# One in-order load queue for activations and weights, weight casts on GpSimd, transposes issued from ScalarE, in a retention plus MLP kernel on one core

## The chip, the cores and the metric

The kernel runs on one core of a Trainium2 chip. The metric is device time in microseconds (us), the median of several executions. Engine names in the profile: PE is TensorE's matmul row, PEld its weight loads, DVE is VectorE, ACT is ScalarE, POOL is GpSimd, SP is SyncE. A name with q (SPq, ACTq) is that engine's instruction queue where it issues DMAs. "L83" is a line of the kernel's file.

## The reference

```python
scores = q @ k.T / sqrt(64)                      # batch 8, heads 8, sequence 576, head_dim 64
ret    = scores * Dmat                           # Dmat[i,j] = gamma_h ** (i-j) for i >= j, else 0
x      = (ret @ v) -> (4608 tokens, 512)
h      = x @ w_in                                # 512 x 2048
g      = h * tanh(softplus(h))                   # "mish"
out    = g @ w_out                               # 2048 x 512, float32
```

Inputs and output are float32. The kernel computes in bf16 with float32 accumulation.

## The kernel before

The 4608 tokens are cut into 36 chunks of 128; four chunks (0 to 3, 4 to 7, ...) make a tile of 512 tokens, nine tiles in all. A chunk goes through four steps: P (GpSimd casts k and scales v, VectorE scales q), T (q and k are transposed), S (score matmuls, mask on VectorE, state matmul) and O (output matmuls, copy into the tile's `xT`). A tile then goes through `g1`, the first MLP layer (16 blocks f of 4 matmuls and one activation on ScalarE), and `g2`, the second layer (16 groups of 4 matmuls, an output copy and a store per chunk). In the main loop, tile t's `g1`, tile t-1's `g2` and the attention of tile t+1 are interleaved.

```python
io  = tile_pool("io",  bufs=8)    # raw q, k, v: 8 chunks deep
tok = tile_pool("tok", bufs=3)    # cast q, k, v of a chunk
op  = tile_pool("op",  bufs=3)    # "res": output copies on their way to HBM
PF = 7
for n in range(PF): load(n)       # each load: 3 DMAs of 256 KB on SyncE's queue
# ... constants ...
def load_w_in(i):                 # float32 -> bf16 in the DMA, on GpSimd's queue
    nc.gpsimd.dma_start(out=w_in_t[:, :, ts(i, 512)], in_=w_in_r[:, :, ts(i, 512)])
# ...
def step_t(n):
    # ...
    if n < NCH:                   # chunks 0 to 3: 8 PE transposes into PSUM, copied by ScalarE
        tp = ps_o.tile([P, 2 * NP, P], BF16, name="ops")
        for i in range(2 * NP):
            nc.tensor.transpose(tp[:, i, :], flat[:, ts(i, P)], ident)
        nc.scalar.copy(qk.rearrange("p i n t -> p (i n) t"), tp)
    else:                         # all others: a DMA transpose, on SyncE's queue
        nc.sync.dma_start_transpose(out=qk.rearrange("p i n t -> p (i n) t"), in_=flat)
# ...
        if step == "P":
            prep(n); step_t(n)
            if n + PF < n_chunks: load(n + PF)
# ...
for i in range(4): load_w_in(i)
for n in range(NCH):
    att(n, "P"); att(n, "S"); att(n, "O")
for i in range(4): load_w_out(i)
att(NCH, "P")
for t in range(nT + 1):
    # per i of 16: P of chunk n+1 and S of chunk n (i%4 == 0), O of n (i%4 == 2), g1(t, i), g2(t-1, i)
```

## Time and profile before

| | before |
|---|---|
| time | 364.15 us median (363.94 to 366.07, 4 runs) |
| span of the profiled run | 362.2 us |
| PE busy | 303.6 us (84%) |
| first MLP matmul | 67.53 us |
| tile 1 begins in the main loop | 88.0 us |

The busy row of PE over the span in 40 equal slices of about 9 us (a digit is tenths), with the TensorE clock that was granted and the mean share of the DMA engines:

```profile
PE   1134200699999999999999999999999999999994
...
PEclk9999999999999999999999999999999999999998
DMA  8999999999866977677777786677322222110022
```

The stretch before the first MLP matmul (7 slices and a bit) is nearly empty on PE while the DMA engines are full. After it PE is busy all the time. The wait that ends this stretch, by the timeline (start us, duration us, engine, line, operation; in brackets the idle time of the engine before it and what ended it):

```profile
62.05 2.21 SPq L166 DMA_TRANSPOSE qkT<-qks  x1
...
66.59 0.61 PE L176 MATMUL sc<-qkT 64*128 64x128 bf16 x8 [27.70 <-DMA qkT<-qks]
...
67.53 1.06 PE L228 MATMUL hp<-xT,w_in_t 128*128 128x512 bf16 x2
```

PE idled 27.7 us before the scores of chunk 4, for chunk 4's DMA transpose (L166). That was issued at 62.05, though its input had been ready since 40.2 (VectorE's scaling of chunk 4's q, from 39.53; GpSimd's cast of its k was done at 33.6): on SyncE's queue it stood behind the loads of chunks up to 10.

In the groups view (busy us and mean ns of one, then the idle time before the group and what ended most of it):

```profile
L228 PE MATMUL hp<-xT,w_in_t 128*128 128x512 bf16 x576 | 148.2, 382 | 0.0
L238 PE MATMUL ops<-w_out_t,gT 128*128 128x512 bf16 x576 | 145.2, 379 | 0.0
...
L176 PE MATMUL sc<-qkT 64*128 64x128 bf16 x288 | 15.4, 231 | 32.5 <-DMA qkT<-qks 28.1
```

The two MLP layers are 1152 matmuls whose starts are 0.216 us apart in a full loop: 249 us that no reordering takes away. What can shrink is the stretch before 67.5.

### The profile page before, as it was taken

The numbers are of one execution on the slowest core, as the hardware profiler recorded it, in microseconds if no ns is written. First come the engines' busy times: TensorE is split into PE (matmuls) and PEld (weight loads), VectorE is DVE, ScalarE is ACT, GpSimd is POOL, SyncE is SP. The second block draws the span as 40 slices with busy tenths as digits, with TensorE's granted clock in tenths as the row PEclk, the third lists the DMA queues.
The fourth block names the chain that finished last, engine by engine and source line by source line (L and its number), as shares of the span: only waits on it lengthen the run. The fifth ranks groups of instructions, "written<-read, shape, count | busy, mean of one in ns | idle before, by whom it ended". The sixth has DMA issues, their size and how long they took to land.

```text
span 362.2 us, 5007 instructions
## 1 busy us (share of the span) xinstructions
PE 303.6 (84%) x2016; PEld 146.7 (40%) x2016; DVE 135.6 (37%) x188; ACT 93.0 (26%) x152; POOL 77.0 (21%) x92
## 2 busy tenths in 40 slices
PE   1134200699999999999999999999999999999994
PEld 1123100354444444444444444444444444444442
DVE  2324400376444444554444444445444444300121
ACT  2012100144322323232322323223322323233300
POOL 7037020133223222222222222222222200000000
PEclk9999999999999999999999999999999999999998
DMA  8999999999866977677777786677322222110022
GB/s 153 196 219 208 194 211 211 222 186 218 162 158 140 200 164 153 147 146 176 171 157 169 169 172 150 147 152 172 80 65 58 61 58 60 29 59 29 29 89 58
DMA packets 155800, 50.67 MB, mean 140 GB/s; under 512 B 147073, under 2 KB 151169, under 8 KB 155777
## 3 DMA queue, kind: packets, MB, share of 16 engines
q1 hardware_dynamic: 151552, 46.15, 61.3%
q0 software_dynamic: 4224, 4.19, 6.9%
q8 instruction: 16, 0.26, 0.3%
q14 instruction: 8, 0.06, 0.1%
HBM read 36.70 MB, written 9.44 MB: 127 GB/s over the span
## 4 chain that ended last, share of the span: by engine, by line
PE 78%; SPq 16%; DMA 3%; issue 1%; DVE 1%; DVEq 0%
PE ops L238 34%; PE hp L228 34%; SPq L83 15%; PE ot L209 3%; PE sc L176 3%; DMA qkT<-qks 3%; PE st L190 3%; PE ot L204 1%; SPq L87 1%; DVE qks L152 0%; DVE res L242 0%; SPq L166 0%; DVEq L152 0%; DVE xT L217 0%
## 5 line engine op out<-in xcount | busy, mean ns | idle before, releaser
L228 PE MATMUL hp<-xT,w_in_t 128*128 128x512 bf16 x576 | 148.2, 382 | 0.0
L238 PE MATMUL ops<-w_out_t,gT 128*128 128x512 bf16 x576 | 145.2, 379 | 0.0
L230 ACT ACTIVATE gT<-hp 128x512 bf16<-128x512 f32 x144 | 86.0, 597 | 220.1 <-PE hp L228 220.1
L238 PEld LDWEIGHTS <-gT 128*128 128x128 bf16 x576 | 56.4, 98 | 68.0
L228 PEld LDWEIGHTS <-w_in_t 128*128 128x128 bf16 x576 | 52.6, 98 | 57.2 <-issue 1.7
L242 DVE COPY res<-ops 128x512 f32<-128x512 f32 x36 | 24.9, 692 | 116.0 <-PE ops L238 110.3
L180 DVE TENSOR_TENSOR sm<-sc,mask 128x1024 bf16<-128x1024 f32 x36 | 43.9, 1220 | 47.8 <-PE sc L176 47.8
L153 POOL TENSOR_TENSOR vs<-vraw,gv 128x512 bf16<-128x512 f32 x36 | 38.0, 1056 | 97.8 <-PE ot L209 74.2
L151 POOL CAST qks<-kraw 128x512 bf16<-128x512 f32 x36 | 31.2, 866 | 113.6 <-PE st L190 76.5
L217 DVE CAST xT<-ot 128x512 bf16<-128x512 f32 x36 | 24.9, 692 | 53.2 <-PE ot L209 52.7
L176 PE MATMUL sc<-qkT 64*128 64x128 bf16 x288 | 15.4, 231 | 32.5 <-DMA qkT<-qks 28.1
L152 DVE TENSOR_TENSOR qks<-qraw,gq 128x512 bf16<-128x512 f32 x36 | 26.5, 737 | 3.5 <-DMA qraw<-in_q_dram 3.5
L176 PEld LDWEIGHTS <-qkT 64*128 64x128 bf16 x288 | 8.7, 99 | 47.0 <-DMA qkT<-qks 28.8
L213 DVE TENSOR_TENSOR ssb<-st,diag 128x512 bf16<-128x512 f32 x32 | 21.8, 682 | 0.0
L163 PE MATMUL ops<-ident,qks 128*128 128x128 bf16 x32 | 4.5, 309 | 19.6 <-DVE qks L152 12.4
L209 PE MATMUL ot<-sm,vs 128*64 128x128 bf16 x288 | 15.8, 234 | 1.9 <-DVE sm L180 1.9
L190 PE MATMUL st<-vs,qks 128*128 128x128 bf16 x128 | 13.8, 235 | 0.0
L209 PEld LDWEIGHTS <-vs 128*64 128x64 bf16 x288 | 10.2, 114 | 7.8 <-issue 5.5
L204 PEld LDWEIGHTS <-ssb 128*128 128x128 bf16 x128 | 9.3, 103 | 5.9
L204 PE MATMUL ot<-qkT,ssb 128*128 128x128 bf16 (+1 forms) x128 | 11.6, 221 | 0.0
L164 ACT COPY qkT<-ops 128x1024 bf16<-128x1024 bf16 x4 | 4.0, 1012 | 29.3 <-PE ops L163 29.3
L163 PEld LDWEIGHTS <-qks 128*128 128x128 bf16 x32 | 2.9, 135 | 20.9 <-DVE qks L152 13.1
(24 smaller groups left out, 20.7 us busy)
## 6 DMA issues: line engine op xcount, KB each, us to landing
qraw<-in_q_dram SPq DMA_DIRECT2D x32, 256.0 KB, 3.9
kraw<-in_k_dram SPq DMA_DIRECT2D x32, 256.0 KB, 4.4
vraw<-in_v_dram SPq DMA_DIRECT2D x32, 256.0 KB, 4.7
out_dram<-res SPq DMA_DIRECT2D x32, 256.0 KB, 2.1
w_in_t<-in_moe_w_in_dram POOLq DMA_DIRECT2D x4, 512.0 KB, 11.8
w_out_t<-in_moe_w_out_dram POOLq DMA_DIRECT2D x4, 512.0 KB, 11.6
qraw<-in_q_dram SPq DMA_DIRECT2D x8, 128.0 KB, 3.4
kraw<-in_k_dram SPq DMA_DIRECT2D x8, 128.0 KB, 3.4
```

Of the source, the lines that this page charges most:

```text
L83: nc.sync.dma_start(out=t, in_=src[b, :, ds(P * c, P), :].rearrange("h p d -> p h d"))
L151: nc.gpsimd.tensor_copy(qks[:, 1], kr)
L152: nc.vector.tensor_tensor(qks[:, 0], qr, gq[:, c, :].unsqueeze(2).to_broadcast([P, H, D]), op=OP.mult)
L153: nc.gpsimd.tensor_tensor(vs, vr, gv[:, c, :].unsqueeze(2).to_broadcast([P, H, D]), op=OP.mult)
L176: nc.tensor.matmul(sc[:, e, p, :], lhsT=qk[r, 1, p, :], rhs=qk[r, 0, p, :], start=True, stop=True)
L180: nc.vector.tensor_tensor(sm.rearrange("p e n i -> p (e n) i"), sc.rearrange("p e n i -> p (e n) i"), m.unsqueeze(1).to_broadcast([P, 2 * ...
L209: nc.tensor.matmul(ot[ds(64 * e, 64), p, :], lhsT=vs[:, 2 * p + e, :], rhs=sm[:, e, p, :], start=(first and p == 0), stop=True, skip_group ...
L217: nc.vector.tensor_copy(xts[t][:, :, ts(s, P)], ot)
L228: nc.tensor.matmul(hp, lhsT=w_in_t[:, c, ts(f, P)], rhs=xts[t][:, c, :], start=(c == 0), stop=(c == KC - 1))
L230: nc.scalar.activation(gts[t][:, f, :], hp, AX.Mish)
L238: nc.tensor.matmul(ops, lhsT=gts[t][:, f, ts(s, P)], rhs=w_out_t[:, f, :], start=(f == 0), stop=(f == nF - 1))
L242: nc.vector.tensor_copy(ot, ops)
```

## The change

Intent: fill the first 67 us. All loads go out in order on one queue, first chunks 0 to 3, then `w_in` in eight pieces of 512 KB, then chunks and `w_out` pieces mixed; the pieces stay float32 and GpSimd casts them. Tile 0 consumes the weights as they come, also in its second layer: four accumulators (two PSUM buffers of `ops` and two of `hp`) take one `w_out` row block after another, while the attention of tile 1 runs. DMA transposes move to ScalarE's queue so as not to stand behind loads. The diff is shortened; `...` marks what is left out or abridged.

```diff
+    stage = ctx.enter_context(tc.tile_pool(name="stage", bufs=STG))      # STG = 4
+    def load_w(nm, i):                 # one 512 KB piece, float32, SyncE's queue
+        t = stage.tile([P, 1024], F32, name="wst")
+        ... nc.sync.dma_start(out=t..., in_=w_in_r[:, :, ts(i, 256)]  or  w_out_r[:, ts(i, 2), :])
+    def cast_w(nm, i):
+        ... nc.gpsimd.tensor_copy(w_in_t[:, :, ts(i, 256)]  or  w_out_t[:, ts(i, 2), :], ...)
-    for n in range(PF):
+    for n in range(NCH):
         load(n)
+    for i in range(STG):
+        load_w("in", i)
...
-            nc.sync.dma_start_transpose(out=qk.rearrange("p i n t -> p (i n) t"), in_=flat)
+            nc.scalar.dma_start_transpose(out=qk.rearrange("p i n t -> p (i n) t"), in_=flat)
...
         if step == "P":
             prep(n)
+            if n >= 2 * NCH - 1 and n + PF < n_chunks:
+                load(n + PF)           # P of chunks 7 and 8 loads chunks 14 and 15
...
+    for i in range(8):
+        cast_w("in", i)
+        if i + STG < 8: load_w("in", i + STG)
+        g1(0, 2 * i); g1(0, 2 * i + 1)
+    load(4); att(4, "P"); att(4, "T")
+    for i in range(STG):
+        load_w("out", i)
+        if i % 2: load(4 + (i + 1) // 2)
+    def more(j, n):
+        cast_w("out", j)
+        if j + STG < 8: load_w("out", j + STG)
+        if j == 1: load(7)
+        elif j == 3:
+            for m in range(2 * NCH, 2 * NCH + 4): load(m)
+        elif j in (4, 6): load(2 * NCH + 2 + j // 2)
+    for f in range(nF):                # second layer of tile 0, with attention of tile 1
+        ... w == 0: more, S(n)   w == 1: P(n+1)   w == 2: more, O(n)   w == 3: T(n+1)
+        for s in range(NCH):
+            nc.tensor.matmul(accs[s], lhsT=gts[0][:, f, ts(s, P)], rhs=w_out_t[:, f, :], ...)
+    for s in (2, 3, 0, 1):             # four output copies and stores of tile 0
+        store(0, s, accs[s], nc.vector.tensor_copy if s % 2 else nc.scalar.copy)
+    for t in range(1, nT + 1):         # the main loop, from tile 1; T(n+1) at i%4 == 1; g2 from t = 2
```

More of the change, by code (lines that the diff above doesn't have):

```diff
@@ L64 @@
     op = ctx.enter_context(tc.tile_pool(name="op", bufs=3))
+    STG = 4
+    stage = ctx.enter_context(tc.tile_pool(name="stage", bufs=STG))
     PS = bass.MemoryType.PSUM
@@ L91, in load @@
         raw[n] = tiles
+    w_in_t = wpool.tile([P, KC, d_ff], BF16)
+    w_out_t = wpool.tile([P, nF, d_model], BF16)
+    w_in_r = moe_w_in.rearrange("(c p) f -> p c f", p=P)
+    w_out_r = moe_w_out.rearrange("(f p) d -> p f d", p=P)
+    staged = {}
+    def load_w(nm, i):
+        t = stage.tile([P, 1024], F32, name="wst")
+        if nm == "in":
+            nc.sync.dma_start(out=t.rearrange("p (c f) -> p c f", c=KC), in_=w_in_r[:, :, ts(i, 256)])
+        else:
+            nc.sync.dma_start(out=t.rearrange("p (f d) -> p f d", f=2), in_=w_out_r[:, ts(i, 2), :])
+        staged[nm, i] = t
+    def cast_w(nm, i):
+        t = staged.pop((nm, i))
+        if nm == "in":
+            nc.gpsimd.tensor_copy(w_in_t[:, :, ts(i, 256)], t.rearrange("p (c f) -> p c f", c=KC))
+        else:
+            nc.gpsimd.tensor_copy(w_out_t[:, ts(i, 2), :], t.rearrange("p (f d) -> p f d", f=2))
     PF = 7
-    for n in range(PF):
+    for n in range(NCH):
         load(n)
+    for i in range(STG):
+        load_w("in", i)
     ident = consts.tile([P, P], BF16)
@@ L126 @@
     nc.vector.memset(diag[64:P, 64:P], 1.0)
-    w_in_t = wpool.tile([P, KC, d_ff], BF16)
-    w_out_t = wpool.tile([P, nF, d_model], BF16)
-    w_in_r = moe_w_in.rearrange("(c p) f -> p c f", p=P)
-    w_out_r = moe_w_out.rearrange("(f p) d -> p f d", p=P)
-    def load_w_in(i):
-        nc.gpsimd.dma_start(out=w_in_t[:, :, ts(i, 512)], in_=w_in_r[:, :, ts(i, 512)])
-    def load_w_out(i):
-        nc.gpsimd.dma_start(out=w_out_t[:, ts(i, 4), :], in_=w_out_r[:, ts(i, 4), :])
     st_ps = {}
@@ L240, in g2, with store @@
         if part == 3:
-            ot = op.tile([P, d_model], F32, name="res")
-            nc.vector.tensor_copy(ot, ops)
-            b, c = chunks[NCH * t + s]
-            if c < 4:
-                nc.sync.dma_start(out=out[ds(b * S + P * c, P), :], in_=ot)
-            else:
-                for e in range(2):
-                    nc.sync.dma_start(out=out[ds((b + e) * S + 512, 64), :], in_=ot[ds(64 * e, 64), :])
+            store(t, s, ops, nc.vector.tensor_copy)
+    def store(t, s, ops, copy):
+        ot = op.tile([P, d_model], F32, name="res")
+        copy(ot, ops)
+        b, c = chunks[NCH * t + s]
+        if c < 4:
+            nc.sync.dma_start(out=out[ds(b * S + P * c, P), :], in_=ot)
+        else:
+            for e in range(2):
+                nc.sync.dma_start(out=out[ds((b + e) * S + 512, 64), :], in_=ot[ds(64 * e, 64), :])
     n_chunks = len(chunks)
@@ L257, in att @@
             prep(n)
+            if n >= 2 * NCH - 1 and n + PF < n_chunks:
+                load(n + PF)
+        elif step == "T":
             step_t(n)
-            if n + PF < n_chunks:
-                load(n + PF)
         elif step == "S":
@@ L264, in att @@
             step_o(n)
-    for i in range(4):
-        load_w_in(i)
     for n in range(NCH):
-        att(n, "P")
-        att(n, "S")
-        att(n, "O")
-    for i in range(4):
-        load_w_out(i)
-    att(NCH, "P")
-    for t in range(nT + 1):
+        for step in "PTSO":
+            att(n, step)
+    for i in range(8):
+        cast_w("in", i)
+        if i + STG < 8:
+            load_w("in", i + STG)
+        g1(0, 2 * i)
+        g1(0, 2 * i + 1)
+    load(4)
+    att(4, "P")
+    att(4, "T")
+    for i in range(STG):
+        load_w("out", i)
+        if i % 2:
+            load(4 + (i + 1) // 2)
+    accs = [ps_o.tile([P, d_model], F32, name="ops") for _ in range(2)]
+    accs += [ps_h.tile([P, NCH * P], F32, name="hp") for _ in range(2)]
+    def more(j, n):
+        cast_w("out", j)
+        if j + STG < 8:
+            load_w("out", j + STG)
+        if j == 1:
+            load(7)
+        elif j == 3:
+            for m in range(2 * NCH, 2 * NCH + 4):
+                load(m)
+        elif j in (4, 6):
+            load(2 * NCH + 2 + j // 2)
+    for f in range(nF):
+        n, w = NCH + f // 4, f % 4
+        if w == 0:
+            more(f // 2, n)
+            att(n, "S")
+        elif w == 1:
+            att(n + 1, "P")
+        elif w == 2:
+            more(f // 2, n)
+            att(n, "O")
+        else:
+            att(n + 1, "T")
+        for s in range(NCH):
+            nc.tensor.matmul(accs[s], lhsT=gts[0][:, f, ts(s, P)], rhs=w_out_t[:, f, :],
+                             start=(f == 0), stop=(f == nF - 1))
+    for s in (2, 3, 0, 1):
+        store(0, s, accs[s], nc.vector.tensor_copy if s % 2 else nc.scalar.copy)
+    for t in range(1, nT + 1):
         for i in range(nF):
@@ L282 @@
                     att(n, "S")
+                elif w == 1:
+                    att(n + 1, "T")
                 elif w == 2:
@@ L285 @@
                 g1(t, i)
-            if t > 0:
+            if t > 1:
                 g2(t - 1, i)
```

## The prediction

> **What bounds it now.** Two phases. The 40-slice view shows PE at 9 tenths from about 68 us on, and nearly nothing before. By the timeline tile 0's first MLP matmul starts at 67.5 us and the second tile's interleaved loop at 88.8; from there PE is 100% busy (stage table: 50.00 of 50.00 us in 200:250), a tile with attention takes about 32.3 us, the matmul chain ends near 357.7, the last store 4.5 us later.
>
> The first 67 us are mostly waiting. Weight loads on the GpSimd queue compete with chunk 1, whose attention starts at 14.7, chunk 0's at 4.2. Attention of four chunks ends at 39.6 (6.1 us each once data is there, a serial chain). Then PE idles 27.7 us, put down in the groups view to "DMA qkT<-qks": the transpose of chunk 4 sits on SyncE's queue behind loads of later chunks and issues at 62.05, landing at 66.5. A 786 KB chunk then takes about 3.5 us (213 GB/s).
>
> **What the change does.** Bytes read stay the same. Weights come as 512 KB fp32 pieces, cast by GpSimd (the 512-element k cast takes 0.61 us alone, 1.01 beside VectorE; estimate for 1024 elements 1.2 to 1.9 us, 16 casts). Transposes no longer queue behind loads, but hold ScalarE 1.24 us each (its SyncE duration; up to 2.7 loaded), in order with the activations.
>
> My timeline, an estimate from these durations:
> - Chunks 0 to 3 land by about 16.5 us, attention ends near 30 (the 6.1 us chain limits, not loading).
> - w_in pieces[...] are cast by about 33, hardly limiting: the first layer of tile 0 runs 30 to 46 (16 x 0.865, plus about 2 cold).
> - Chunk 4's transpose stands behind the last activation on ScalarE: issued near 47, landed near 50.5: PE idles 4 us and restarts cold. The Trainium skill ("TensorE: Matmul & The Clock Gate", Part 1) says the clock halves after about 3.4 us idle; this trace agrees: six matmuls took 2.75 us at 67.5, later 0.216 each.
> - Second layer of tile 0 with attention of tile 1: 4.8 us of PE work per chunk, but the next transpose waits for q-scale after the mask (2.5 us) and lands 3.2 to 5 us later, so 6 to 6.5 us per chunk. It ends near 76. w_out's last cast is near 66: weights limit less than this chain.
> - Tile 1's first layer alone: 4.8 us of work, 6 with the transpose on ScalarE: until about 101.
> - Then six full tiles (194), 27.7, 13.9 and the 4.5 tail: 240.
>
> Sum 341 us of span; time exceeds span by 1.7, but my stalls are rounded up: 341.5. So about 27.7 us of MLP second-layer and overlapped attention work moves into time that was idle, and some 5 to 8 us are given back as transpose latency. The steady loop should be unchanged: its transpose has 8 us per chunk.
>
> **Predicted: 341.5 us, 80% range 333 to 350. Faster by over 2%: 0.95; within 2%: 0.04; slower: 0.01.**
>
> **Signs.** Right: first MLP matmul near 30 us; idle before score matmuls released by the qkT transpose of some 4 us once and 1 to 2 us per chunk until about 100; span after that equal to before; few waits of PE on w_in or w_out casts. Wrong: accumulating matmuls waiting on GpSimd casts (weights limit), or the interleaved loop over 8.1 us per chunk (ScalarE held up).
>
> **What would break it.** Transposes landing in 6 us or more beside a full load queue (350); weight pieces slower than the 213 GB/s of chunks (345); GpSimd casts over 2 us, delaying k and v; or transposes landing in 3 us and pieces fast (333).

## More of the kernel before

The kernel before ran beside every set of experiments, with medians of 364.15 to 365.05 us, so a difference between runs of different sets carries about 1 us.

## The result

| | before | after |
|---|---|---|
| time, median (range) | 364.15 us (363.94 to 366.07) | 374.35 us (373.54 to 375.25) |
| ratio to before | | 1.0269 (95% interval 1.0226 to 1.0311) |
| first MLP matmul | 67.53 | 29.51 |
| end of tile 0's second layer | in the main loop | 78.0 |
| interleaved loop begins (full tile) | 88.0 | 130.3 |
| PE busy | 303.6 us | 311.9 us |
| mean granted clock | 0.997 | 0.950 |

It is slower. Ratios here and below are the mean time of one kernel's fast runs over that of the other's fast runs of the same rounds, so not quite the ratio of the medians.

The 40 slices of the changed kernel (9.3 us each):

```profile
PE   2458928744056799999999999999999999999995
...
PEclk9999958995569999999999999999999999999999
DMA  9999997599999828787986789899222322101022
```

PE now starts in slice 4 as intended, but a second hole opened: slices 9 to 12, about 78 to 112 us. The timeline around it, without the matmuls (columns as before):

```profile
78.18 0.58 ACT L259 COPY res<-hp 128x512 f32<-128x512 f32 x1 [31.53 <-PE hp L330]
78.40 0.69 DVE L259 COPY res<-hp 128x512 f32<-128x512 f32 x1 [1.14 <-PE hp L330]
78.66 0.59 ACT L259 COPY res<-ops 128x512 f32<-128x512 f32 x1
...
83.17 0.61 PE L190 MATMUL sc<-qkT 64*128 64x128 bf16 x8 [4.81 <-DMA qkT<-qks]
...
99.08 5.20 SPq L262 DMA_DIRECT2D out_dram<-res  x4
103.23 0.69 DVE L259 COPY res<-ops 128x512 f32<-128x512 f32 x1 [24.15 <-DMA out_dram<-res]
...
104.44 1.22 DVE L194 TENSOR_TENSOR sm<-sc,mask 128x1024 bf16<-128x1024 f32 x1
...
105.71 0.59 PE L223 MATMUL ot<-sm,vs 128*64 128x128 bf16 x7 [17.98 <-DVE sm L194]
```

Tile 0 has four output copies. The first three ran at 78.2 to 79.2. The fourth, on VectorE, started only at 103.23: VectorE stood still for 24.15 us, and what released it is "DMA out_dram<-res", the first output store, which had been issued at 99.08. There are three `res` buffers, so the fourth copy needs the first store to have landed. VectorE took its work in program order: the mask of chunk 8 (L194), whose scores PE had computed from 83.17 on, stood behind that copy and ran at 104.44, and PE's output matmuls of chunk 8 (L223) waited 17.98 us for the mask.

Why were stores of copies made at 78 issued at 99? SyncE issues in program order too, and the program places the loads of chunks 8 to 15 before the stores. They would have been issued sooner, had this queue not stood still three times. These are its DMA issues at the ends of the gaps, by the timeline of SyncE:

```profile
53.09 1.87 SPq L89 DMA_DIRECT2D kraw<-in_k_dram  x2
67.27 1.27 SPq L89 DMA_DIRECT2D vraw<-in_v_dram  x2
68.65 0.57 SPq L85 DMA_DIRECT2D qraw<-in_q_dram  x1
73.47 0.37 SPq L85 DMA_DIRECT2D kraw<-in_k_dram  x1
...
77.62 1.37 SPq L85 DMA_DIRECT2D qraw<-in_q_dram  x1
83.14 0.37 SPq L85 DMA_DIRECT2D kraw<-in_k_dram  x1
...
97.90 1.09 SPq L85 DMA_DIRECT2D vraw<-in_v_dram  x1
99.08 5.20 SPq L262 DMA_DIRECT2D out_dram<-res  x4
```

Between 54.96 and 67.27, 69.22 and 73.47, 78.99 and 83.14 it issued nothing. These three gaps are 20.7 us. The waits view of SyncE names what ended them (total us, times, longest); two of the five waits, of 5.8 and 0.6 us, came after the stores:

```profile
SPq L85 <- DMA qkT<-qks: 14.1, 3, 5.8
SPq L89 <- DMA qkT<-qks: 12.9, 2, 12.3
```

The chain of work shows when these transposes landed (start, duration, so the end of each is the landing: 67.25, 73.46, 83.12):

```profile
64.21 3.04 DMA qkT<-qks
...
69.73 3.73 DMA qkT<-qks
...
75.84 7.28 DMA qkT<-qks
```

Each time the next load went out 0.01 to 0.02 us after a DMA transpose landed. A load of v for chunk 8 has no data in common with the transpose of chunk 6. The built program says why it waits. Its DMAs on the two queues take eight completion semaphores in turn (the columns: place in the order, queue, what it writes, the count it waits for, the semaphore that it raises by 16):

```
40  ACT  qkT of chunk 6                  ...            DMAHW0 (to 96)
48  SP   vraw of chunk 8 (first half)    DMAHW0 >= 96   DMAHW0
44  ACT  qkT of chunk 7                  ...            DMAHW4 (to 96)
52  SP   kraw of chunk 9                 DMAHW4 >= 96   DMAHW4
50  ACT  qkT of chunk 8                  ...            DMAHW2 (to 112)
58  SP   kraw of chunk 11                DMAHW2 >= 112  DMAHW2
72  SP   out (first store of tile 0)     DMAHW0 >= 144  DMAHW0
```

A DMA first waits until the DMA eight places ahead has landed, on whichever queue that is. Transposes wait for PE and VectorE (T(n+1) needs q of chunk n+1, which VectorE scales after the mask of chunk n), so through the shared semaphores the loads wait for compute, the stores wait for the loads, and VectorE for the stores.

The waits view of the engines (total us, times, longest) shows this chain in its first and last line, and in the middle one a smaller loss:

```profile
DVE res L259 <- DMA out_dram<-res: 24.1, 1, 24.1
...
PE sc L190 <- DMA qkT<-qks: 20.8, 8, 7.1
PE ot L223 <- DVE sm L194: 19.9, 5, 18.0
```

PE waited 20.8 us for transposes. Of these 7.1 + 1.5 + 0.7 + 1.4 + 4.8 = 15.5 us lie before the scores of chunks 4 to 8, as brackets of those matmuls in the timeline say: a transpose took up to 7.3 us to land here. In the steady loop (130 to 280 us) the median is 3.1 us in the kernel before and 5.7 in the changed one.

The loop from tile 2 on is unchanged: it ran from 130.3 to the last matmul's start at 367.6, 237 us, where I had 235.6 (194 + 27.7 + 13.9); in the kernel before, from 120.15 to 357.3, it is 237 us too. Nor did PE wait for weights: the waits view has no wait of PE on a weight cast.

### The profile page after: what moved, and what is told of

The parts are those of the page before. It is cut to its first block, busy times and chain, and to the rows that moved or that the text cites. A ratio compares the mean times of both kernels' runs of the same rounds, so it can differ in the third digit from the quotient of the medians.

```text
span 372.4 us, 5097 instructions
## 1 busy us (share of the span) xinstructions
PE 311.9 (84%) x2016; PEld 148.8 (40%) x2016; DVE 134.2 (36%) x186; ACT 93.9 (25%) x154; POOL 85.5 (23%) x100
## 4 chain that ended last, share of the span: by engine, by line
PE 66%; DMA 18%; SPq 10%; issue 3%; DVE 2%; POOL 1%; ACTq 1%; ACT 0%; DVEq 0%; POOLq 0%
PE ops L252 30%; PE hp L242 27%; DMA qkT<-qks 12%; SPq L85 9%; DMA wst<-in_moe_w_in_dram 3%; PE sc L190 3%; PE ot L223 2%; PE st L204 2%; DMA vraw<-in_v_dram 2%; PE ot L218 1%; DMA out_dram<-res 1%; DVE qks L166 1%; POOL w_in_t L113 1%; ACTq L180 1%; SPq L105 0%
## 5 line engine op out<-in xcount | busy, mean ns | idle before, releaser
L242 PE MATMUL hp<-xT,w_in_t 128*128 128x512 bf16 x576 | 150.6, 392 | 1.3 <-DVE xT L231 0.8
L252 PE MATMUL ops<-w_out_t,gT 128*128 128x512 bf16 x512 | 128.8, 379 | 0.0
L242 PEld LDWEIGHTS <-w_in_t 128*128 128x128 bf16 x576 | 54.0, 100 | 63.3 <-issue 9.0
L252 PEld LDWEIGHTS <-gT 128*128 128x128 bf16 x512 | 50.1, 98 | 60.4
L259 DVE COPY res<-ops 128x512 f32<-128x512 f32 x33 | 22.8, 691 | 128.8 <-PE ops L252 104.7
L194 DVE TENSOR_TENSOR sm<-sc,mask 128x1024 bf16<-128x1024 f32 x36 | 43.9, 1219 | 51.8 <-PE sc L190 51.8
L165 POOL CAST qks<-kraw 128x512 bf16<-128x512 f32 x36 | 29.1, 807 | 101.5 <-PE st L204 60.7
L190 PE MATMUL sc<-qkT 64*128 64x128 bf16 x288 | 15.6, 233 | 25.2 <-DMA qkT<-qks 20.8
L223 PE MATMUL ot<-sm,vs 128*64 128x128 bf16 x288 | 16.3, 239 | 19.9 <-DVE sm L194 19.9
L223 PEld LDWEIGHTS <-vs 128*64 128x64 bf16 x288 | 10.6, 116 | 26.2 <-issue 23.8
L330 PE MATMUL ops<-w_out_t,gT 128*128 128x512 bf16 x32 | 10.6, 417 | 0.0
L330 PE MATMUL hp<-w_out_t,gT 128*128 128x512 bf16 x32 | 10.4, 411 | 0.0
```

The lines of the kernel that those rows point to most:

```text
L165: nc.gpsimd.tensor_copy(qks[:, 1], kr)
L190: nc.tensor.matmul(sc[:, e, p, :], lhsT=qk[r, 1, p, :], rhs=qk[r, 0, p, :], start=True, stop=True)
L194: nc.vector.tensor_tensor(sm.rearrange("p e n i -> p (e n) i"), sc.rearrange("p e n i -> p (e n) i"), m.unsqueeze(1).to_broadcast([P, 2 * ...
L223: nc.tensor.matmul(ot[ds(64 * e, 64), p, :], lhsT=vs[:, 2 * p + e, :], rhs=sm[:, e, p, :], start=(first and p == 0), stop=True, skip_group ...
L242: nc.tensor.matmul(hp, lhsT=w_in_t[:, c, ts(f, P)], rhs=xts[t][:, c, :], start=(c == 0), stop=(c == KC - 1))
L252: nc.tensor.matmul(ops, lhsT=gts[t][:, f, ts(s, P)], rhs=w_out_t[:, f, :], start=(f == 0), stop=(f == nF - 1))
```

## Experiments

Theory Q: the queue order and the three buffers make VectorE wait for a store (24 us). Theory L: the loads wait for transposes through the shared semaphores. Rivals: A, transposes held up ScalarE; C, the loss is TensorE's lower clock (0.950 against 0.997), not a wait. A fifth question is what each part of the change is worth by itself. All edits are to the changed kernel unless said otherwise.

### Four output buffers

```diff
-    op = ctx.enter_context(tc.tile_pool(name="op", bufs=3))
+    op = ctx.enter_context(tc.tile_pool(name="op", bufs=4))
```

> Edit: four output buffers (res) in place of three. Theory Q (queue order and buffers): in the changed kernel VectorE stands 24 us (79.1 to 103.2) before the fourth output copy, because the first output store is behind the loads of chunks 9 to 15 on SyncE's queue and only three buffers exist; with a fourth buffer the copy needs no store, so tile 1's attention goes on at about 83.5 in place of 104.4: time 349 to 356, the 24 us wait of VectorE on the output store gone, the stores themselves still near 100 us. Rival A (ScalarE held by transposes): the wait only shows where the engines stand, time stays over 365. Rival C (PE clock, granted 0.95): time follows the clock; a fourth buffer does not change it, over 365.

Measured: 356.49 us (355.12 to 357.52), ratio to before 0.9789; half a us above my range. VectorE's wait on the store is gone, though the first store went out even later, at 100.9. The scores of chunks 8 and 9, by the timeline of PE:

```profile
82.53 0.61 PE L190 MATMUL sc<-qkT 64*128 64x128 bf16 x8 [4.91 <-DMA qkT<-qks]
...
90.27 0.40 PE L190 MATMUL sc<-qkT 64*128 64x128 bf16 x8 [1.52 <-DMA qkT<-qks]
```

Tile 1's first scores are where they were, but the next chunk's follow at 90.27, not at 110.61. This shows Q, and speaks against A and C: nothing about ScalarE or the clock was touched, and 17.9 us went. The mean clock rose to 0.978 by itself, which fits a low clock that follows from PE's waits. The clock figure alone proves little: in the kernel before, the first MLP matmuls start 0.43 us apart from 67.5 to 70.1, twice the later 0.216, but the windows view gives a granted clock of 1.00 there.

### Stores before the late loads

```diff
         elif j == 3:
-            for m in range(2 * NCH, 2 * NCH + 4):
+            for m in range(2 * NCH, 2 * NCH + 2):
                 load(m)
-        elif j in (4, 6):
-            load(2 * NCH + 2 + j // 2)
 ...
-            if n >= 2 * NCH - 1 and n + PF < n_chunks:
+            if n >= 2 * NCH + 1 and n + PF < n_chunks:
 ...
         store(0, s, accs[s], ...)
+    for m in range(2 * NCH + 2, 4 * NCH):
+        load(m)
```

> Edit: three output buffers as in the changed kernel, but the loads of chunks 10 to 15 are issued after tile 0's four stores in place of before them. Theory Q: stores issue near 79 and land near 82, VectorE waits under 3 us, tile 1 goes on near 80 to 82: time 346 to 354, at or below the run with four buffers. Rivals A and C: over 365.

Measured: 358.30 us (354.04 to 359.32), ratio 0.9819: the direction of Q, but 4 us above the range that I gave. The stores went out at 79.6, as expected. The waits of this run tell where the rest went:

```profile
POOL qks L165 <- DMA kraw<-in_k_dram: 35.6, 13, 8.8
...
PE sc L190 <- DMA qkT<-qks: 24.1, 11, 8.0
...
DVE res L259 <- DMA out_dram<-res: 8.7, 2, 6.7
```

Of VectorE's 8.7 us on stores, the fourth copy of tile 0 waited only 2.0 (it ran at 81.91), within the 3 that I had expected; the other 6.7 us ended at 147.6, in the steady loop. GpSimd waited 35.6 us for k (21.9 in the changed kernel, 24.3 with four buffers), since the loads of chunks 10 and later are now issued later, and PE waited 24.1 us for transposes (20.8 and 23.7). The times of this run and of the one with four buffers overlap, so which edit is the better one isn't shown.

### Transposes of chunks 4 to 8 on PE

```diff
-        else:
+        elif n < 2 * NCH + 1:
+            tp = ps_sc.tile([P, 4 * NP, P], BF16, name="sc")[:, 0:2 * NP, :]
+            for i in range(2 * NP):
+                nc.tensor.transpose(tp[:, i, :], flat[:, ts(i, P)], ident)
+            nc.scalar.copy(qk.rearrange("p i n t -> p (i n) t"), tp)
+        else:
```

> Edit: chunks 4 to 8 are transposed on PE through PSUM and copied by ScalarE, as chunks 0 to 3 are; nothing else. Theory L (loads wait for transposes: the DMAs of both queues share eight completion semaphores in turn, so a load waits until the DMA eight before it has landed, and that is at times a transpose that itself waits for PE): SyncE's waits on qkT, 27 us in the changed kernel, vanish, loads run on without the gaps at 55 to 67, 69 to 73 and 79 to 83, so the last load before the stores goes out near 82 in place of 99. PE's idle time before scores in tile 1's attention (15.4 us) falls under 3. The second layer of tile 0 ends near 70 in place of 78, but VectorE still waits for the first store, until about 85: time 352 to 360. If L is wrong, stores stay near 99 and the time stays near 374.

Measured: 359.91 us (358.40 to 360.77), ratio 0.9881. The waits view of SyncE in this run:

```profile
SPq L85 <- DMA qkT<-qks: 6.2, 1, 6.2
```

And VectorE's wait in the same run, by the waits view of the engines:

```profile
DVE res L264 <- DMA out_dram<-res: 18.3, 1, 18.3
```

The three gaps on SyncE are gone: it issues loads without a pause from 46 to 83.6, and the first store at 83.67 in place of 99.08. What is left of its waits on qkT, 6.2 us, is one, later in the run. The scores of chunks 5 to 8 come 5.4 to 5.6 us apart with 0.3 us of idle before each, and chunk 8's at 69.06 in place of 83.17. So L holds. But VectorE still waited 18.3 us for the store, as foreseen: tile 0 is done earlier, and the loads are still ahead of its stores.

### Transposes back on SyncE's queue

```diff
-            nc.scalar.dma_start_transpose(...)
+            nc.sync.dma_start_transpose(...)
```

> Edit: the transposes are issued from SyncE's queue again, all else of the change kept. Rival A (ScalarE's queue is the fault): the loss vanishes, time near 345. Theories Q and L: chunk 4's transpose goes out earlier (near 32, not behind the last activation), later ones stand behind loads of chunks 8 to 15, stores still behind all loads, issued near 84 to 95; time 352 to 370, less than the changed kernel's 374 by some but with a VectorE wait of over 8 us on the first store left.

Measured: 370.34 us (368.26 to 372.32), ratio 1.019, just above my range. Against rival A this is plain: with no transpose on ScalarE the loss to the kernel before stays. The wait has another place here: PE waited 12.2 us before chunk 6's scores and 8.0 before chunk 5's, for transposes that stand behind loads, and VectorE only 4.2 us for a store, where I had expected over 8.

### Four buffers and transposes of chunks 4 to 8 on PE

> Edit: four output buffers, and chunks 4 to 8 transposed on PE, so tile 1's first layer still has DMA transposes from ScalarE's queue. Theory: tile 0's second layer ends near 69, tile 1's loop has 6 to 7 us per chunk as in the changed kernel: tile 2 begins near 95, time 336 to 344. The difference to the run with chunks 4 to 12 on PE is what the DMA transposes cost in tile 1's loop, expected 3 to 6 us.

Measured: 344.73 us, the median of four with one slow run (348.61); the three fast ones are 343.33, 343.65 and 345.80, ratio 0.9447. Alone, the two edits gave 17.9 and 14.4 us; together, by the median of the fast runs, 30.7. The difference to the next run (336.20) is 7.5 us, more than the 3 to 6 that I had expected.

### Four buffers and transposes of chunks 4 to 12 on PE

```diff
-    op = ...(name="op", bufs=3)
+    op = ...(name="op", bufs=4)
...
+        elif n < 3 * NCH + 1:                   # PE transposes through ps_sc, as above
...
-                elif w == 1:
+                elif w == 1 and t > 1:
                     att(n + 1, "T")
                 elif w == 2:
                     att(n, "O")
+                    if t == 1:
+                        att(n + 1, "T")
```

> Edit to the changed kernel: four output buffers, and chunks 4 to 12 transposed on PE (in tile 1's loop the transposes stand after the output step); DMA transposes from chunk 13 on. Theories Q and L say the two causes add: second layer of tile 0 ends near 69 us, no VectorE wait on stores, tile 1's first layer 5.3 us per chunk, tile 2's loop begins near 90 (130 in the changed kernel), then the unchanged 244: 332 to 338. If the causes do not add or another limit stands behind them (weights or loads), over 342.

Measured: 336.20 us (335.21 to 336.91), ratio to before 0.9223. It beats both kernels: 28 us under the one before, 38 under the changed one. By the timeline of PE, the first score matmuls of chunk 4, of chunk 8, and of chunk 12, where the loop of tile 2 begins:

```profile
46.76 0.40 PE L195 MATMUL sc<-qkT 64*128 64x128 bf16 x8 [1.16 <-ACT qkT L183]
...
68.93 0.40 PE L195 MATMUL sc<-qkT 64*128 64x128 bf16 x8 [0.30 <-ACT qkT L183]
...
89.85 0.40 PE L195 MATMUL sc<-qkT 64*128 64x128 bf16 x8
```

The changed kernel has these three at 53.16, 83.17 and 130.3. Tile 2's loop begins at 89.9, I had said 90.

### The same with three buffers

> Edit to the run with four buffers and chunks 4 to 12 on PE (336.2 us): three output buffers again. No DMA transpose is left for the loads to wait on, but tile 0's stores still stand behind the loads of chunks 8 to 15 on SyncE's queue, which run until about 82: VectorE waits from about 70 to 84 to 86 for the first store, time 347 to 354. If the buffer wait only exists together with the shared semaphores, the time stays at 336.

Measured: 354.36 us (354.13 to 355.31), ratio 0.9721, 0.4 us above my range. VectorE's wait is back without any transpose that loads could wait on:

```profile
DVE res L264 <- DMA out_dram<-res: 16.8, 1, 16.8
```

So the two causes stand separately, and here they add: from the changed kernel (374.35), the fourth buffer alone takes 17.9 us, PE transposes for chunks 4 to 12 alone take 20.0, both take 38.2.

### The weights part undone alone

From the 336.2 us kernel, with the weights loaded as in the kernel before:

```diff
-    (weight pieces on SyncE's queue, cast by GpSimd)
+    for i in range(4):
+        nc.gpsimd.dma_start(out=w_in_t[:, :, ts(i, 512)], in_=w_in_r[:, :, ts(i, 512)])
     for n in range(NCH): ...
+    for i in range(4):
+        nc.gpsimd.dma_start(out=w_out_t[:, ts(i, 4), :], in_=w_out_r[:, ts(i, 4), :])
```

> Edit to the 336.2 us kernel: weights again as eight casting DMAs of 512 columns or 4 row blocks on GpSimd's queue, as in the kernel before; so the first part of the change (one in-order load queue, cast by GpSimd) is undone alone. Chunk 1 then waits for w_in as before (q at 14.7 in place of 11), chunk 3's attention ends near 38 to 40 in place of 29.5, and the later steps shift with it: 343 to 348. If the order of the weights does not matter, 335 to 338.

Measured: 343.08 us (341.67 to 344.98), ratio 0.9410. The first MLP matmul of tile 0 comes at 37.63 in place of 29.49. Chunk 1 is late again: GpSimd waits 10.3 us for its k while the `w_in` DMAs run, and its scores come at 20.40 in place of 13.95. The weights in order on the load queue, cast by GpSimd, are worth about 7 us.

### The transposes part of the change alone

The kernel before, with `nc.sync.dma_start_transpose` made `nc.scalar.dma_start_transpose`, one word.

> One part of the change alone: the kernel before, with only the transposes moved to ScalarE's queue. Chunk 4's transpose no longer stands behind the loads, but in the built program it waits for the load eight DMAs ahead (k of chunk 5, landed at 49.9 before), so scores of chunk 4 near 54 in place of 66.6: time 346 to 358. If queue order alone mattered, and not the shared completion semaphores, scores near 44 and time 340 to 345.

Measured: 351.35 us (350.61 to 351.99), ratio 0.9641: one word takes 13 us. Chunk 4's scores, by the timeline:

```profile
42.56 7.21 ACTq L166 DMA_TRANSPOSE qkT<-qks  x2
42.61 0.61 POOL L151 CAST qks<-kraw 128x512 bf16<-128x512 f32 x1 [8.35 <-DMA kraw<-in_k_dram]
...
50.30 0.61 PE L176 MATMUL sc<-qkT 64*128 64x128 bf16 x8 [13.40 <-DMA qkT<-qks]
```

They come at 50.3 in place of 66.6. I had expected 54, and 44 if the semaphores played no part. The time lies between my two values, but the trace tells the parts of the delay. The input of chunk 4's transpose was ready at 38.2 (the scaling of its q; its k was cast by 33.3). In the built program the transpose also waits for the k load of chunk 5, and that landed at 42.5: GpSimd's cast of this k (second line) begins at 42.61, and the transpose went out at 42.56. Chunk 5's transpose, which waits for the v load of chunk 5 in the same way, went out at 48.51, 0.10 us after that v landed. So the semaphore cost chunk 4's transpose 4.4 us, and the landing beside the loads took another 7.7, in place of 4.5 in the kernel before.

### The kernel before with PE transposes for chunks 4 to 8

```diff
-        if n < NCH:
+        if n < 2 * NCH + 1:
```

> The kernel before with chunks 4 to 8 transposed on PE, nothing of the change: if its 27.7 us of PE idle at 39 to 66.6 is only the transpose behind the loads, tile 0's first layer starts near 43 to 46, is then limited by chunk loads (chunks 5 to 8 land 3.6 us apart, 50 to 61), and ends near 66 to 70 in place of 88.4: time 342 to 348.

Measured: 356.32 us (356.04 to 357.33), ratio 0.9783; I missed by 8 us. The 27.7 us of idle time did vanish: chunk 4's scores come at 43.36, chunk 8's at 68.87. But a new wait stood behind it:

```profile
82.28 1.77 SPq L166 DMA_TRANSPOSE qkT<-qks  x1
...
86.05 0.61 PE L176 MATMUL sc<-qkT 64*128 64x128 bf16 x8 [9.08 <-DMA qkT<-qks]
```

Chunk 9 has the first DMA transpose now, and it too stands on SyncE's queue behind the loads, which had meanwhile run ahead. PE idled 9.1 us for it. In both kernels the first transpose on that queue pays.

### A software pipeline over the first four chunks

From the 336.2 us kernel: P of chunk n+1 before S of chunk n, T of n+1 before O of n, for chunks 0 to 3.

> Edit to the 336.2 us kernel: in the first four chunks the prep and transposes of chunk n+1 are placed before the mask and output of chunk n, so the 6.1 us serial chain per chunk becomes about 4: first layer of tile 0 starts near 21 to 23 in place of 29.5, is then limited by the w_in casts (last at 31.8) and ends near 37 in place of 45; the second layer then meets w_out (last cast with chunk 8, near 58 to 62): time 327 to 334.

Measured: 334.07 us (332.70 to 336.77), ratio 0.9169. The runs overlap with those of the 336.2 us kernel, so a gain of some 2 us is not certain. The first MLP matmul came at 22.03 in place of 29.49, but only about 2 us of these 7.5 arrived at tile 2's loop (87.86 in place of 89.85), mainly because the second layer now waits for weight casts:

```profile
PE ops L341 <- POOL w_out_t L115: 4.0, 3, 1.9
```

This is the only run in which PE waits for weight casts. The weights themselves had landed: the piece whose cast ran from 49.06 on was in SBUF at 43.2, but GpSimd, in program order, first cast the k and scaled the v of chunk 6 and waited for their loads (2.6 and 1.4 us).

## Why the prediction was wrong

- **"First MLP matmul near 30 us": right.** 29.51. Chunks 0 to 3 were processed in 6.1 us each, `w_in`'s last cast began at 30.8 (I had said by 33), a cast took 1.04 us (estimate 1.2 to 1.9).
- **"Chunk 4's transpose stands behind the last activation ... PE idles 4 us": right in kind, 7.1 us in size.** Issued at 46.20, scores at 53.16.
- **"Second layer of tile 0 ... ends near 76": nearly right, 78.0.** The chain of q-scale, transpose and scores set it, as I had said.
- **"w_out's last cast is near 66": wrong, it began at 72.7.** I had assumed that the load queue never pauses. It paused for transposes through the shared semaphores: the cast stood on GpSimd behind the scaling of chunk 8's v, which waited 8.4 us for a load that was issued only at 67.27. It did not cost PE time here by way of the weights, but it is the first sign of the step that failed.
- **"Tile 1's first layer alone: 4.8 us of work, 6 with the transpose on ScalarE: until about 101": this step failed.** It ended at 130.3. From the scores of chunk 8 it took 47.1 us in place of 24 to 25. My sum had no term for tile 0's four stores at all. The term that was missing is a wait of VectorE, 24.15 us, for an output buffer: stores behind loads on SyncE's queue, and three buffers for four copies. The experiments put 17.9 to 18.2 us on it (four buffers in place of three, with and without DMA transposes before chunk 13).
- **Transposes "land 3.2 to 5 us later": too small beside a full queue.** They took up to 7.3 us to land, and the loads that waited for them moved back. DMA transposes in place of PE transposes, for chunks 4 to 12, cost 20.0 us in the changed kernel and 20.3 with four buffers, of which I had counted "5 to 8" us. I had named landings of 6 us or more as a risk, but priced it at 350 us. The two terms together, 17.9 us and the 12 to 15 not counted here, are 30 to 33 us, and the prediction missed by 32.9.
- **"The steady loop should be unchanged": right.** 237 us against 235.6.
- **What I gave as signs of being wrong** (matmuls waiting on casts, ScalarE held up in the loop) did not happen. I had looked at the engines that the change loads, and not at the queue that it reorders: each DMA placed on an in-order queue also delays what stands behind it, and a full set of loads was placed before the stores.
- The Trainium skill's "TensorE: Matmul & The Clock Gate", Part 1, which I cited, agrees with the after trace too: after 4.8 us of idle time chunk 8's scores ran at 0.61 us per eight matmuls, after 1.5 us (chunk 5) at 0.40. The bound is blurred in other runs: with the transposes back on SyncE's queue, chunk 8's scores still took 0.40 us after 4.3 us of idle time, and the matmuls were 0.43 us apart only from 95.7 on, 1 us later. The mean clock of 0.950 goes with the waits: it is 0.998 in the 336.2 us run.

What stays open: why a transpose takes longer to land on ScalarE's queue. The one word that moves it there raises the median landing in the steady loop (130 to 280 us) from 3.1 to 5.8 us with the same loads. On SyncE's queue a transpose is issued in turn with the loads, on ScalarE's beside loads in flight; that this is the reason is not shown by any run here.

## What to carry to other kernels

When a change gathers transfers on one in-order queue, write down for each queue what now stands behind what, stores and buffer counts included: a copy that needs a free output buffer waits for a store, and the store for every load ahead of it. Look in the built program which completion semaphores the DMAs share, because a load can wait for an unrelated transpose on another engine's queue. A buffer more (one line, 17.9 us here) is worth trying before the order of a schedule is given up; the change's own idea was sound, and with a fourth buffer and without the DMA transposes of chunks 4 to 12 it is 28 us faster than the kernel before.

## What the Trainium skill lacked or had wrong

- "DMA: Bandwidth & Descriptors", section "Issuing engines are not separate DMA queues", says that initiating DMAs on several engines "will only save the time on the sequencer it takes to initiate the DMA, which is usually small relative to the DMA itself". Here the move of the transposes alone from SyncE's to ScalarE's queue took 13 us off (364 to 351), because chunk 4's transpose was issued 19.5 us earlier (42.56 in place of 62.05): the order on a queue, and what its head waits for, is part of the matter, and the section doesn't speak of it.
- No page has that the DMAs of a built program can share a small set of completion semaphores in turn (eight here), so that one waits for another eight places ahead on a different queue. It held SyncE's queue for 27.0 us in the changed kernel (14.1 + 12.9), 20.7 of it before the stores of tile 0.
- "DMA: Bandwidth & Descriptors", section "Latency and other measured facts", gives a bandwidth for DMA transposes, but no time to landing beside other traffic. Here 256 KB took 3.0 to 7.3 us from issue to landing, the median 5.5 in the changed kernel and 3.2 in the one before.
